# An attention and gated-MLP kernel rewritten: projections one head group ahead, wide normalization, transposes on the DMA queue, a Gelu activation, streamed weights

## The chip, the cores and the metric

The kernel runs on one core of one Trainium2 chip. The metric is the device time of one execution, in microseconds. In the profile, PE is TensorE (matmuls), PEld its weight loads, DVE is VectorE, ACT is ScalarE, POOL is GpSimd and SP is SyncE, which here only issues DMAs. "PEclk" or "clock" is the TensorE clock granted, as a share of full speed.

## The reference

Two pre-norm blocks on 2048 tokens of width 1024, in bf16. Cut to what matters:

```python
def _A_ref(x, wq, wk, wv, wo, beta):          # 32 heads of 32, 4 segments of 512 tokens
    q, k, v = x @ wq, x @ wk, x @ wv          # split into heads and segments
    for s in range(4):
        logits = q_s @ k_s.T * scale + causal_mask
        a_dot = softmax(logits) @ v_s
        a_mem = (phi(q_s) @ M) / (phi(q_s) @ z + 1e-6)   # phi(t) = t+1 if t>0 else exp(t)
        o_s = g * a_mem + (1 - g) * a_dot                # g = sigmoid(beta), one per head
        M, z = M + phi(k_s).T @ v_s, z + sum(phi(k_s))
    return o @ wo
def _B_ref(x, w_in, w_sp, b_sp, w_out):
    z = gelu_tanh(x @ w_in)                   # 1024 -> 3584
    z1, z2 = z[..., :1792], layernorm(z[..., 1792:])
    return (z1 * (w_sp @ z2 + b_sp)) @ w_out  # w_sp: 2048 x 2048 over tokens
h = x + _A_ref(layernorm(x)); out = h + _B_ref(layernorm(h))
```

## The kernel before

Work on each engine is one queue in program order; semaphores join the queues. Four stages follow each other: segment 0 is projected; then for each segment eight groups ("quads") of four heads, with the projections of the next segment as filler, and an output projection at the end of the segment; then the gated input projection; then the spatial product and the output. PV is the product of the exponentials with the values. A bank is one of the eight pieces of the memory in which TensorE leaves its results. z1 and z2 are the two halves of the gated input projection; a z2 chunk is one tile of 128 tokens by 1792 columns.

The logits of one block of keys; the causal mask is added by matmuls with a constant:

```python
def L(j):                                   # j = 0..3, widths 512, 384, 256, 128
    for i in range(4):                      # four heads, four row groups, banks 0-3
        pe.matmul(bank(i)[:, 0:nj], kT[32*i:..., keys j], qT[32*i:..., 128*j:512], start=True, stop=False)
    for i in range(4):
        pe.matmul(bank(i)[:, 0:128], IDENT, NEGTRI, start=False, stop=True)
    act.activation(ESALL[:, :, OFFJ[j]:...], PS[:, 0:4, 0:nj], Exp, scale=SCALE)
# ... PV_emit(cq) for each of four query blocks, then on VectorE, each on 128 columns or fewer:
    dM += eps; RD = 1/[dA, dM]; RD *= GG; TA = A*RD; TM = Mn*RD; otok = TA + TM   # six small operations
```

One block of the gated input projection, on two buffers of each kind. The factor 2 that remains in z is taken out later:

```python
w = [bank free] ; if z2 block and fb == 0: w.append(z2g_res.free)   # previous chunk normalized
tp = proj8(...)                                                     # 8 matmuls, 512 columns
t1 = act.activation(X2T[g], ps, Square)
t2 = dve.scalar_tensor_tensor(WG[g], X2T[g], GELU_K, ps, add, mult)
t3 = act.activation(TH[g], WG[g], Tanh, scale=GELU_C)               # one block later
t4 = dve.scalar_tensor_tensor(out, TH[g], 1.0, ps, add, mult)
# after four z2 blocks: layer norm of the 1792 columns in Z2G, a single buffer
```

The softmax here doesn't subtract the row's maximum and nothing guards it: scores larger than these inputs give would overflow.

Of the kernel before, what the change touches and what calls it, by code (L numbers as in the profile page):

```python
# [5 lines left out]
BF16 = mybir.dt.bfloat16  # L6
# [5 lines left out]
T = 2048  # L12
D = 1024
H = 32
DH = 32
# [6 lines left out]
SCALE = DH ** (-0.5)  # L22
LN_EPS = 1e-5
MEM_EPS = 1e-6
GELU_C = 0.7978845608028654 * 0.044715
GELU_K = 1.0 / 0.044715
NJ = [512, 384, 256, 128]
OFFJ = [0, 512, 896, 1152]
ESLOT = 1280


class _Sig:

    def __init__(self, sem, name):
        self.sem = sem
        self.name = name
        self.n = 0


class _Plan:  # L40
    ENG = ("pe", "act", "dve", "pool", "sp")

    def __init__(self):
        self.ops = {k: [] for k in self.ENG}
        self.waited = {k: {} for k in self.ENG}

    def op(self, eng, fn, waits=(), sig=None):
        w = []
        for item in waits:
            if item is None:  # L50
                continue
            s, v = item
            if v <= 0:
                continue
            if self.waited[eng].get(s.name, 0) >= v:
                continue
            self.waited[eng][s.name] = v
            w.append((s.sem, v))
        semobj = None
        if sig is not None:  # L60
            sig.n += 1
            semobj = sig.sem

        def run(e, fn=fn, w=tuple(w), semobj=semobj):
            for (sm, v) in w:
                e.wait_ge(sm, v)
            ins = fn(e)
            if semobj is not None:
                ins.then_inc(semobj, 1)

        self.ops[eng].append(run)
        return (sig, sig.n) if sig is not None else None

    def dma(self, eng, dst, src, sem16, waits=(), transpose=False):
        w = []
        for item in waits:
            if item is None:
                continue
            s, v = item
            if v <= 0:  # L80
                continue
            if self.waited[eng].get(s.name, 0) >= v:
                continue
            self.waited[eng][s.name] = v
            w.append((s.sem, v))
        sem16.n += 1

        def run(e, dst=dst, src=src, w=tuple(w), semobj=sem16.sem, transpose=transpose):
            for (sm, v) in w:
                e.wait_ge(sm, v)  # L90
            e.dma_start(dst, src, transpose=transpose).then_inc(semobj, 16)

        self.ops[eng].append(run)
        return (sem16, sem16.n)


class _DmaSig(_Sig):
    pass


def _w16(tok):
    if tok is None:
        return None
    s, v = tok
    return (s, 16 * v) if isinstance(s, _DmaSig) else (s, v)


def bass_sequential_preLN__memory_aug_infini_attn__mixer_gmlp__prompt_kernel(
# [16 lines left out]
    plan = _Plan()  # L125
    P = plan.op

    sem_handles = []

    def mksig(name, dma=False):  # L130
        h = nc.alloc_semaphore(name)
        sem_handles.append(h)
        return (_DmaSig if dma else _Sig)(h, name)

    g_pool = mksig("g_pool")
    g_dve_pe = mksig("g_dve_pe")
    g_dve_act = mksig("g_dve_act")
    g_dve_sp = mksig("g_dve_sp")
    g_dve_pool = mksig("g_dve_pool")
    g_dve_dve = mksig("g_dve_dve")  # L140
    g_act_dve = mksig("g_act_dve")
    g_act_pe = mksig("g_act_pe")
    g_act_act = mksig("g_act_act")
    g_pe_act = mksig("g_pe_act")
    g_pe_dve = mksig("g_pe_dve")
    d_w3 = mksig("d_w3", True)
    d_wo = mksig("d_wo", True)
    d_win = mksig("d_win", True)
    d_wout = mksig("d_wout", True)
    d_beta = mksig("d_beta", True)  # L150
    d_x = [mksig("d_x0", True), mksig("d_x1", True)]
    d_xr = [mksig("d_xr0", True), mksig("d_xr1", True)]
    d_hr = [mksig("d_hr0", True), mksig("d_hr1", True)]
    d_wsp = [mksig("d_wsp0", True), mksig("d_wsp1", True)]
    d_brow = [mksig("d_brow0", True), mksig("d_brow1", True)]
    d_out = [mksig("d_out0", True), mksig("d_out1", True)]

    ARENA = 209920 + 2048
    arena = nc.alloc_sbuf_tensor("arena", [128, ARENA], mybir.dt.uint8)
    abase = nc.lookup_mloc(arena).addr  # L160
    _cur = [0]

    def region(size):
        off = _cur[0]
        _cur[0] += size
        assert _cur[0] <= ARENA, ("arena overflow", _cur[0])
        return off

    def tens(name, shape, dt, off):
        sz = int(np.prod(shape[1:])) * mybir.dt.size(dt)  # L170
        assert off % 32 == 0, (name, off)
        assert off + sz <= ARENA, (name, off, sz)
        return nc.alloc_sbuf_tensor_at(name, list(shape), dt, offset=abase + off)

    R_CONST = region(4096)
    R_WQKV = region(49152)
    R_PK = region(16384)
    R_WO = region(16384)
    R_XNT = region(8192)
    R_QT = region(16384)  # L180
    R_KT = region(16384)
    R_PQT = region(16384)
    R_V = region(17408)
    R_E = region(10240)
    R_OTOK = region(8192)
    R_OT = region(8192)
    R_XCH = region(4096)
    R_XN = region(2048)
    R_XR = region(4096)
    R_HCH = region(4096)  # L190
    R_QTMP = region(4096)
    R_NORM = region(4096)
    R_XN2 = region(2048)
    assert _cur[0] == ARENA

    c = R_CONST
    IDENT = tens("ident", [128, 128], BF16, c); c += 256
    TRI = tens("tri", [128, 128], BF16, c); c += 256
    GG = tens("gg", [128, NQ, 8], F32, c); c += 256
    BETAB = tens("betab", [128, H], BF16, c); c += 64  # L200
    G32 = tens("g32", [128, 2, H], F32, c); c += 256
    MSUM = tens("msum", [128, NQ, 33], F32, c); c += 1056
    c = (c + 31) // 32 * 32
    MZ = tens("mz", [128, NQ, 34], BF16, c); c += 544
    STATS = tens("stats", [128, 4, 6], F32, c); c += 96
    MV = tens("mv", [128, 2], F32, c); c += 32
    SM4 = tens("sm4", [128, 8], F32, c); c += 32
    MHALF = tens("mhalf", [128, 1], F32, c); c += 32
    RD = tens("rd", [128, 8], F32, c); c += 32
    SUMS = tens("sums", [128, 8], F32, c); c += 32  # L210
    IOT = tens("iot", [128, 128], I32, c); c += 512
    NEGTRI = tens("negtri", [128, 128], BF16, c); c += 256
    assert c <= R_CONST + 4096

    WQKV = tens("wqkv", [128, 3, 8, D], BF16, R_WQKV)
    PKS = [tens("pk0", [128, 4, D], BF16, R_PK), tens("pk1", [128, 4, D], BF16, R_PK + 8192)]
    WO = tens("wo", [128, 8, D], BF16, R_WO)
    XNT = tens("xnT", [128, 8, L], BF16, R_XNT)
    QTS = [tens("qT0", [128, NQ, L], BF16, R_QT), tens("qT1", [128, NQ, L], BF16, R_QT + 8192)]
    KTS = [tens("kT0", [128, NQ, L], BF16, R_KT), tens("kT1", [128, NQ, L], BF16, R_KT + 8192)]  # L220
    PQTS = [tens("pqT0", [128, NQ, L], BF16, R_PQT), tens("pqT1", [128, NQ, L], BF16, R_PQT + 8192)]
    VS = [tens("v0", [128, 4, H, 34], BF16, R_V), tens("v1", [128, 4, H, 34], BF16, R_V + 8704)]
    ES = [tens("e%d" % i, [128, ESLOT], BF16, R_E + i * 2560) for i in range(4)]
    ESALL = tens("eall", [128, 4, ESLOT], BF16, R_E)
    OTOK = [tens("otok%d" % i, [128, D], BF16, R_OTOK + i * 2048) for i in range(4)]
    OT = tens("oT", [128, NQ, L], BF16, R_OT)
    XCH = [tens("xch%d" % i, [128, D], BF16, R_XCH + i * 2048) for i in range(2)]
    XN = [tens("xn0", [128, D], BF16, R_XN), tens("xn1", [128, D], BF16, R_XN2)]
    XR = [tens("xr%d" % i, [128, D], BF16, R_XR + i * 2048) for i in range(2)]
    HCH = [tens("hch%d" % i, [128, D], BF16, R_HCH + i * 2048) for i in range(2)]  # L230
    TMPE = tens("tmpe", [128, D], BF16, R_QTMP)
    QE = tens("qe", [128, L], BF16, R_QTMP + 2048)
    TA = tens("ta", [128, 4, 32], F32, R_NORM)
    TM = tens("tm", [128, 4, 32], F32, R_NORM + 512)
    MZBD = [tens("mzbd%d" % i, [128, 512], BF16, R_NORM + 1024 + i * 1024) for i in range(2)]

    WIN_LO = tens("w_in_lo", [128, 8, FH], BF16, R_WQKV)
    WIN_HI = tens("w_in_hi", [128, 8, FH], BF16, R_WQKV + 28672)
    HNT = [tens("hnT0", [128, 8, L], BF16, R_WO), tens("hnT1", [128, 8, L], BF16, R_WO + 8192)]
    Z1T = tens("z1T", [128, 14, T], BF16, R_XNT)  # L240
# [17 lines left out]
    WSPCH[1] = tens("wspch1", [128, T], BF16, R_CT2 + 5120)  # L258

    PS = nc.alloc_psum_tensor("ps", [128, 8, 512], F32)  # L260

    def bank_f32(b):
        return PS[:, b, :]

# [792 lines left out]
```

## Time and profile before

Median 1267.4 us (1266.9 to 1271.2, 4 runs). Stages of the profiled execution (1264.5 us):

| stage | us |
|---|---|
| start: weights, projections of segment 0 | 71 |
| attention, projections of segments 1 to 3, output projections | 507 |
| layer norm of h, gated input projection | 351 |
| spatial product and output (22 us of it getting started) | 335.5 |

The page of before: busy time by engine, then busy tenths of TensorE and its clock in 40 slices of the span.

```profile
PE 978.3 (77%) x6735; PEld 490.3 (39%) x6848; DVE 672.3 (53%) x1688; ACT 361.8 (29%) x502; POOL 35.1 (3%) x68
...
PE   3978785888669856674858676758639999999998
...
PEclk9979897998879986567978888889869999999999
```

TensorE is nearly full only in the last ten slices, and in most of the slices in which it is not full its clock is lower too (not in the first).

Busy time by window, before. Columns: window, its length, busy us (and instructions) of each engine, clock, DMA share, GB/s.

```profile
core 0: us, PE busy (x) PEld busy (x) DVE busy (x) ACT busy (x) POOL busy (x), PEclk, DMA share, GB/s
0.00:71.00 71.00, 48.16 (x248) 23.68 (x254) 22.50 (x48) 18.69 (x29) 8.31 (x22) 1.00 0.39 141
71.00:578.00 507.00, 381.94 (x3850) 207.92 (x3906) 281.65 (x984) 216.03 (x233) 8.15 (x14) 0.83 0.11 37
578.00:598.00 20.00, 4.61 (x34) 3.41 (x36) 12.09 (x29) 0.00 (x0) 2.20 (x4) 0.60 0.29 93
598.00:929.00 331.00, 234.27 (x1035) 106.48 (x1053) 234.56 (x449) 125.96 (x239) 15.33 (x28) 0.86 0.03 9
929.00:951.00 22.00, 7.51 (x65) 6.87 (x67) 7.50 (x11) 1.13 (x3) 1.12 (x1) 0.50 0.82 296
951.00:1264.50 313.50, 301.81 (x1508) 141.90 (x1533) 113.95 (x168) 0.00 (x0) 0.00 (x0) 0.99 0.15 47
```

In attention TensorE idles 125 of 507 us at a clock of 0.83; in the input projection it idles 97 of 331 us. The timeline inside that stage shows: the four operations of one block follow each other across two engines, and a block comes every 1.99 us (644.47 to 646.46), while its 8 matmuls need 8 x 0.217 = 1.74 (a run of 8 matmuls of 512 columns takes 1.74 us in this trace; 0.217 is used for one throughout).

```profile
644.47 0.63 ACT L828 ACTIVATE th_117<-wg_115 128x512 bf16<-128x512 bf16 x1 [0.87 <-DVE wg_115 L862]
645.01 0.58 ACT L860 ACTIVATE x2t_111<-ps 128x512 bf16<-128x512 f32 x1
645.14 0.69 DVE L833 SCALAR_TENSOR_TENSOR z1T<-th_117,ps 128x512 bf16<-128x512 bf16 x1
645.74 0.68 DVE L862 SCALAR_TENSOR_TENSOR wg_114<-x2t_111,ps 128x512 bf16<-128x512 bf16 x1
646.46 0.63 ACT L828 ACTIVATE th_116<-wg_114 128x512 bf16<-128x512 bf16 x1 [0.87 <-DVE wg_114 L862]
```

The chain that ended last, by engine, before:

```profile
PE 48%; DVE 31%; ACT 11%; issue 4%; DMA 4%; POOL 2%; SPq 0%; DVEq 0%; ACTq 0%; POOLq 0%
```

### The profile page before, as it was taken

How to read it: one execution, taken by the hardware profiler on the slowest of the kernel's cores; microseconds unless marked ns; L12 is line 12 of the kernel's file. 1: busy time of each engine (PE TensorE's matmuls, PEld its weight loads, DVE VectorE, ACT ScalarE, POOL GpSimd, SP SyncE). 2: the span in 40 equal slices, each digit the busy share in tenths (PEclk: the TensorE clock that was granted, in tenths of full speed). 3: DMA queues.
4: the chain of work that ended last, by engine and by line, in shares of the span. 5: the costliest groups of instructions: out<-in, count | busy, mean ns of one | idle time of the engine just before them, and what ended most of it. 6: DMA issues, size and time to landing. Idle time of an engine off the chain costs nothing.

```text
span 1264.5 us, 16478 instructions
## 1 busy us (share of the span) xinstructions
PE 978.3 (77%) x6735; PEld 490.3 (39%) x6848; DVE 672.3 (53%) x1688; ACT 361.8 (29%) x502; POOL 35.1 (3%) x68
## 2 busy tenths in 40 slices
PE   3978785888669856674858676758639999999998
PEld 1444443443334423332423233323224445444443
DVE  4165426864577425654676777776644434244242
ACT  0357523663146405520334243334410000000000
POOL 2000000000000000000000000000000000000000
PEclk9979897998879986567978888889869999999999
DMA  8000012000300070002000000000042030120201
GB/s 315 1 26 1 1 34 68 1 1 1 101 1 2 2 282 18 1 18 91 18 17 1 17 18 9 9 1 1 1 179 83 5 109 26 50 88 5 68 1 59
DMA packets 23308, 54.56 MB, mean 43 GB/s; under 512 B 2368, under 2 KB 6976, under 8 KB 23232
## 3 DMA queue, kind: packets, MB, share of 16 engines
q1 hardware_dynamic: 19152, 34.10, 8.3%
q0 software_dynamic: 4080, 19.40, 4.1%
q8 instruction: 54, 0.88, 0.3%
q14 instruction: 22, 0.18, 0.0%
HBM read 45.10 MB, written 8.39 MB: 42 GB/s over the span
## 4 chain that ended last, share of the span: by engine, by line
PE 48%; DVE 31%; ACT 11%; issue 4%; DMA 4%; POOL 2%; SPq 0%; DVEq 0%; ACTq 0%; POOLq 0%
PE ps L391 16%; PE ps L945 15%; PE ps L972 8%; DVE stats L328 5%; ACT eall L525 4%; DVE z2g L833 3%; DVE z1T L833 3%; ACT th_116 L828 3%; DVE wg_114 L862 3%; DVE wg_115 L862 3%; ACT th_117 L828 3%; PE ps L518 2%; PE ps L511 2%; POOL sm_58 L333 2%; DMA wqkv<-in_A_wv_dram 2%
## 5 line engine op out<-in xcount | busy, mean ns | idle before, releaser
L525 ACT ACTIVATE eall<-ps 128x2048 bf16<-128x2048 f32 (+3 forms) x128 | 158.6, 1239 | 170.8 <-PE ps L518 170.1
L391 PE MATMUL ps<-xnT,wqkv 128*128 128x512 bf16 x489 | 118.8, 388 | 11.4 <-DVE msum L640 4.5
L972 PE MATMUL ps<-w_out,yT 128*128 128x512 bf16 x437 | 96.8, 379 | 6.9 <-DVE yT L951 6.4
L948 DVE TENSOR_TENSOR tmpg<-ps,brow_126 128x512 f32<-128x512 f32 x56 | 38.7, 691 | 117.5 <-PE ps L945 102.6
L945 PE MATMUL ps<-wspT_119,z_106 128*128 128x512 bf16 x439 | 98.2, 384 | 1.7 <-DVE wspT_119 L922 1.3
L945 PE MATMUL ps<-wspT_120,z_106 128*128 128x512 bf16 x440 | 96.6, 379 | 0.4
L391 PE MATMUL ps<-w_in_hi,hnT_104 128*128 128x512 bf16 (+1 forms) x253 | 63.1, 416 | 36.2 <-DVE z_106 L791 36.1
L391 PE MATMUL ps<-w_in_hi,hnT_103 128*128 128x512 bf16 (+1 forms) x251 | 63.4, 419 | 31.4 <-DVE z_106 L791 29.7
L391 PE MATMUL ps<-wo,oT 128*128 128x512 bf16 x248 | 63.4, 410 | 21.6 <-DVE oT L657 21.4
L828 ACT ACTIVATE th_116<-wg_114 128x512 bf16<-128x512 bf16 (+1 forms) x60 | 36.9, 615 | 134.9 <-DVE wg_114 L862 134.9
L391 PEld LDWEIGHTS ps<-xnT,wqkv 128*128 128x128 bf16 x512 | 47.4, 99 | 62.8 <-DVE msum L640 5.7
L972 PEld LDWEIGHTS ps<-w_out,yT 128*128 128x128 bf16 x448 | 43.5, 98 | 60.2 <-DVE yT L951 8.2
L945 PEld LDWEIGHTS ps<-wspT_119,z_106 128*128 128x128 bf16 x448 | 43.9, 99 | 53.2 <-issue 2.5
L945 PEld LDWEIGHTS ps<-wspT_120,z_106 128*128 128x128 bf16 x448 | 43.7, 98 | 51.9
L391 PE MATMUL ps<-wqkv,xnT 128*128 128x512 bf16 x248 | 58.7, 390 | 3.4 <-DVE msum L640 2.6
L518 PE MATMUL ps<-negtri,ident 128*128 128x128 bf16 x512 | 61.3, 255 | 0.0
L391 PEld LDWEIGHTS ps<-w_in_hi,hnT_104 128*128 128x128 bf16 x256 | 27.8, 111 | 73.2 <-DVE z_106 L791 39.6
L391 PE MATMUL ps<-hnT_103,w_in_lo 128*128 128x512 bf16 x218 | 52.4, 396 | 3.2 <-DVE z2g L833 3.0
L391 PEld LDWEIGHTS ps<-w_in_hi,hnT_103 128*128 128x128 bf16 x256 | 28.1, 112 | 68.3 <-DVE z_106 L791 32.7
L828 ACT ACTIVATE th_117<-wg_115 128x512 bf16<-128x512 bf16 (+1 forms) x60 | 35.2, 587 | 67.4 <-DVE wg_115 L862 67.4
L391 PE MATMUL ps<-hnT_104,w_in_lo 128*128 128x512 bf16 x217 | 51.1, 388 | 1.7 <-DVE z2g L833 1.3
L577 DVE TENSOR_SCALAR ps<-ps 128x4 f32<-128x4 f32 x96 | 16.1, 167 | 67.4 <-PE ps L556 64.4
(145 smaller groups left out, 1313.3 us busy)
## 6 DMA issues: line engine op xcount, KB each, us to landing
wspch_121<-in_B_w_sp_dram SPq DMA_DIRECT2D x8, 512.0 KB, 4.2
wspch_128<-in_B_w_sp_dram SPq DMA_DIRECT2D x8, 512.0 KB, 4.3
hr_0_127<-out_dram SPq DMA_DIRECT2D x16, 256.0 KB, 2.8
w_in_lo<-in_B_w_in_dram POOLq DMA_DIRECT2D x1, 3584.0 KB, 12.4
w_in_hi<-in_B_w_in_dram POOLq DMA_DIRECT2D x1, 3584.0 KB, 21.5
w_out<-in_B_w_out_dram POOLq DMA_DIRECT2D x1, 3584.0 KB, 17.9
xch_87<-in_A_x_dram SPq DMA_DIRECT2D x8, 256.0 KB, 2.8
xch_88<-in_A_x_dram SPq DMA_DIRECT2D x8, 256.0 KB, 3.0
```

Of the source, the lines that this page charges most:

```text
L328: t = P("dve", (lambda e, ci=ci: e.bn_stats(STATS[:, ci, :], eng_in_ap[:, ci * csz:(ci + 1) * csz])), waits=((list(first_wait) + [chain["l ...
L333: tp = P("pool", lambda e: e.tensor_tensor(SM4[:, 1:2], SM4[:, 0:1], MHALF[:], ALU.pow), waits=[t], sig=g_pool)
L391: tok = P("pe", (lambda e, i=i: e.matmul(dst, lhs_of_i(i), rhs_of_i(i), start=(i == 0), stop=(i == 7))), waits=(waits if i == 0 else []), ...
L511: P("pe", (lambda e, i=i, dst=dst: e.matmul(dst, kT[32 * i:32 * (i + 1), c, j * 128:(j + 1) * 128], qT[32 * i:32 * (i + 1), c, 128 * j:512 ...
L518: tp = P("pe", (lambda e, dstd=dstd: e.matmul(dstd, IDENT[:], NEGTRI[:], start=False, stop=True)), sig=(g_pe_act if i == 3 else None))
L525: ta = P("act", (lambda e: e.activation(dst4, src4, ACTF.Exp, scale=float(SCALE))), waits=wa, sig=g_act_pe)
L828: t3 = P("act", (lambda e, g=g, ncols=ncols: e.activation(TH[g][:, 0:ncols], WG[g][:, 0:ncols], ACTF.Tanh, scale=float(GELU_C))), waits=[p ...
L833: t4 = P("dve", (lambda e, g=g, ncols=ncols, dst=dst, o=prev["out"]: e.scalar_tensor_tensor(o, TH[g][:, 0:ncols], 1.0, dst, ALU.add, ALU.m ...
L862: t2 = P("dve", (lambda e, g=g, ncols=ncols, dst=dst: e.scalar_tensor_tensor(WG[g][:, 0:ncols], X2T[g][:, 0:ncols], float(GELU_K), dst, AL ...
L945: tok = P("pe", (lambda e, sc=sc, fc=fc, dst=dst: e.matmul(dst, Z2[:, sc, fc * 128:(fc + 1) * 128], wb[:, sc, :], start=(sc == 0), stop=(s ...
L948: t1 = P("dve", lambda e, dst=dst: e.tensor_tensor(TMPG[:], dst, BROW[0][:], ALU.add), waits=[tok, _w16(tb), tmpg_res.free], sig=g_dve_pe)
L972: tok = P("pe", (lambda e, fc=fc, half=half, tcl=tcl, dst=dst: e.matmul(dst, YT[:, fc, tcl * 128:(tcl + 1) * 128], WOUT[:, fc, half * 512: ...
```

## The change

The intent is to keep TensorE fed. Nearly all of the file is new, so the diff is given as its core; helper code (a recorder that places the waits) is cut.

```diff
 # --- attention, one of 32 head groups n
-L(0); extra; L(1); PV(0); extra; L(2); PV(1); extra; L(3); PV(2); PV(3); state; rest of extras
+logits(n, 0)                               # keys 0, 512 columns
+proj_qk(n + 1, 1)                          # K of the NEXT group
+pv(n - 1, 2)                               # last part of the previous group, then its norm
+bg_pop()                                   # background: layer norm of an x or h tile
+logits(n, 1)                               # keys 1 and 3 share the banks, one exponential
+proj_qk(n + 1, 0)                          # Q of the next group
+pv(n, 0); logits(n, 2); fill(f3); phi(n + 1); pv(n, 1); bg_pop(); state(n); fill(f4); bg_pop()
+# fill = a value projection, or an output projection of the previous segment
 # --- causal mask
-4 x pe.matmul(bank, IDENT, NEGTRI) for each block of keys
+pool.affine_select(out=d, in_=d, ..., fill=0.0)            # on the exponentials, in SBUF
 # --- normalization: per query block 128 columns -> all four at once
+dve.reciprocal(RD, PVA[:, :, :, 32]); RD *= OMG; TA = PVA * RD (512 columns); ot = TA + TM
 # --- transposes (normalized x, h, attention output, phi(K), spatial weights)
-pe.transpose(...) x8; dve.tensor_copy(dst, bank)
+sp.dma_start_transpose(dst[:, :, tile], src)
 # --- gated input projection, w_in streamed through three buffers
-Square, (x2 + K) * x, Tanh, (1 + t) * x
+act.activation(z, PS[:, b, 0:448], ACTF.Gelu_apprx_tanh); dve.bn_stats(ZST[...], z)
 # --- start
-pool.dma_start of wq, wk, wv, wo; all of segment 0 projected before attention
+act.dma_start of wv (first half), wk, wq, wv (second half), wo; attention starts when group 0 is projected
```

## The prediction

> **What bounds the kernel now** (table of busy time by window):
> - 0 to 71 us: weights land (first projection matmul at 25.9 us, released by the last weight load), then segment 0 is projected alone, 45 us.
> - 71 to 578 us: attention and output projections. TensorE is busy 76 to 82% in segments 0 to 2 at a granted clock of 0.88, and 62% at 0.57 in segment 3, which has no projections to fill with. Per group of four heads the timeline shows 14 to 15 us: TensorE, four exponentials (1.88, 1.45, 1.02, 0.60 us) and 24 small VectorE operations of 0.17 to 0.29 us take turns. Each segment end costs 19 to 25 us for the output projection alone.
> - 578 to 929 us: layer norm with nothing to overlap (28 us), then the gated input projection, 323 us, although its 896 matmuls need 896 x 0.217 = 194 us. The chain of waits runs through VectorE and ScalarE: square, multiply, tanh, multiply, 0.6 to 0.7 us each, on two buffers.
> - 929 to 950 us: waiting for the transposed spatial weights. 950 to 1264 us: TensorE at clock 0.99, 302 of 314 us busy.
>
> **What changes, costed from the trace**
> - Gated input projection: one Gelu activation (0.6 us) replaces four operations (2.6 us). TensorE (1.74 us per block) becomes the bound: 194 us, plus the last output projection mixed in (64 x 0.217 = 14 us) and about 9 us of bubbles: 217 instead of 351 (578 to 929).
> - Start: value projections begin when half of one weight has come; the first attention group starts at about 25 us instead of 71.
> - Attention: TensorE per group, from durations: Q and K 3.5, V and output projection 0 to 3.5, logits 1.3, PV 1.6, memory and state 0.9 (estimate): 8.5 in segment 0, 10.7 in 1 and 2, 9.4 in 3. The mask matmuls (0.40 us for four, 16 per group) and transposes leave. ScalarE: 7.6 us; VectorE about 7.3. TensorE-bound with 0.5 to 1 us of bubbles: 345 us, with the output projections inside, instead of 507.
> - Final stage: transposes (16.6 us of TensorE and the 21 us start) go to the DMA queue; 896 + 448 matmuls are 292 us, plus block ends: 303 instead of 335.
> - Added: DMA transposes, some 22 MB, 13 MB of them during attention, about 38 GB/s. The Trainium skill's "Advanced Engine Details and Errata", section X-Bar Transpose, calls them as fast as regular DMAs; no trace here shows one. All have several us of slack in program order. Also four GpSimd selects per group[...], off the chain.
>
> Sum: 25 + 345 + 217 + 303 = 890 us. Nearly all of it is on the critical path, because TensorE becomes the chain.
>
> **Prediction: 890 us, 850 to 955 (8 in 10). Faster by over 2%: 0.97; within 2%: 0.015; slower: 0.015.**
>
> **What would show it.** TensorE busy above 90% in nearly all slices and clock near 1.0; chain of waits over 80% TensorE; input projection stage about 215 us; groups of 9 to 11 us in attention; first exponential at about 25 us.
>
> **What would make it wrong.** DMA transposes far slower than plain copies, or blocking the SyncE queue that issues loads in order (TensorE idle, released by DMA); GpSimd selects of 2 us or more, which would put exponential, select and PV on the chain; the loop through banks 0 to 3 (logits, exponential, logits) or the two spare banks leaving TensorE idle, so that groups stay at 12 us and the clock drops: then 940 to 980.

## More of the kernel before

What TensorE waited for, before (total us, times, longest): the normalization of a z2 chunk, and the exponentials.

```profile
PE ps L391 <- DVE z_106 L791: 65.7, 12, 6.4
PE ps L511 <- ACT eall L525: 50.7, 47, 2.0
```

## The result, and the profile after

After: median 867.3 us (865.7 to 870.2, 4 runs). The ratio to before is 0.684, 95% interval 0.682 to 0.687; ratios can differ a little from the ratio of the medians.

The same lines of the page, after:

```profile
PE 802.0 (93%) x5354; PEld 390.6 (45%) x5440; DVE 382.9 (44%) x777; ACT 302.2 (35%) x351; POOL 121.8 (14%) x234
...
PE   1787988899889999699999999999999999999998
...
PEclk9998999999999999899999999999999999999999
```

Busy time by window, after; the windows are the start, attention, the input projection and the final stage.

```profile
0.00:38.20 38.20, 14.93 (x79) 7.20 (x80) 11.82 (x31) 8.78 (x13) 4.38 (x18) 1.00 0.70 247
38.20:363.50 325.30, 289.77 (x2945) 151.34 (x2992) 203.32 (x483) 225.26 (x219) 101.30 (x176) 0.97 0.33 74
363.50:572.60 209.10, 208.49 (x1014) 100.70 (x1026) 68.71 (x122) 67.59 (x119) 16.13 (x40) 0.99 0.23 58
572.60:865.90 293.30, 288.81 (x1318) 131.41 (x1343) 99.06 (x144) 0.60 (x1) 0.00 (x0) 1.00 0.26 65
```

The chain that ended last, after:

```profile
PE 78%; DVE 7%; ACT 5%; POOL 3%; DMA 3%; ACTq 2%; issue 2%; SPq 1%
```

| stage | before | predicted | after |
|---|---|---|---|
| start | 71 | 25 | 38.2 |
| attention and what it holds | 507 | 345 | 325.3 |
| input projection with layer norm | 351 | 217 | 209.1 |
| final stage | 335.5 | 303 | 293.3 |
| sum | 1264.5 | 890 | 865.9 |

The borders shift work a little: attention now also holds most of segment 0's projections (144 of 192 matmuls, 31 us at 0.217 us each), and the last segment's output projection (64 matmuls, 14 us) went into the input projection stage. In attention TensorE is busy 92 us less, and idles 35.5 instead of 125 us. The input projection idles 0.6 of 209 us. Some matmul records are missing from this trace: its attention has 2945, that of the kernel with four operations below, which has the same attention, has 2992 and shows 294.7 us busy of 322.8. So the 35.5 us may be some 5 too many, and the busy time 5 too few.

Two places are still not full. First, the start. The timeline of after, 2 to 20 us; ACTq lines are the time in which ScalarE's queue sat in issuing a DMA:

```profile
1.92 2.40 ACTq L209 DMA_DIRECT2D wq<-in_A_wq_dram  x1
4.34 7.89 ACTq L209 DMA_DIRECT2D wv<-in_A_wv_dram  x1
12.26 5.31 ACTq L209 DMA_DIRECT2D wo<-in_A_wo_dram  x1
17.60 1.28 ACT L209 ACT_TABLE_LOAD   x1 [17.60 <-issue]
18.89 1.02 ACT L209 ACTIVATE xnT_71<-ps 128x1024 bf16<-128x1024 bf16 x1
19.97 2.32 PE L209 MATMUL ps<-wv,xnT_71 128*128 128x512 bf16 x5 [11.54 <-ACT xnT_71 L209]
```

ScalarE could copy nothing out of a bank before 18.9 us, although TensorE had the first transposed tile done at 8.4 us. Second, the head of a segment. The timeline of after, 115 to 123 us, cut to one chain:

```profile
115.71 1.88 ACT L209 ACTIVATE e_100<-ps 128x2048 bf16<-128x2048 f32 x1
...
115.88 0.58 SPq L209 DMA_DIRECT2D xch_88<-in_A_x_dram  x1
...
118.89 1.42 DVE L209 BATCH_NORM_STATS2 stats_59<-xch_88 128x6 f32<-128x512 bf16 x2 [2.23 <-DMA xch_88<-in_A_x_dram]
...
120.94 0.57 POOL L209 TENSOR_TENSOR rs_63<-rs_63,mhalf 128x1 f32<-128x1 f32 x1
...
121.47 1.40 POOL L209 TENSOR_SCALAR_AFFINE_SELECT e_100<-e_100 128x512 bf16<-128x512 bf16 x2
...
122.16 0.27 PE L209 MATMUL ps<-v,e_100 128*128 128x33 bf16 x4 [1.71 <-POOL e_100 L209]
```

The exponentials were ready at 117.6 us, but their select stood in GpSimd's queue behind the power of a layer norm, which waited for an x tile that had only just been asked for. In all, TensorE waited for selects (the operation on GpSimd that sets the masked exponentials to zero):

```profile
PE ps L209 <- POOL e_100 L209: 16.9, 21, 3.3
```

### The profile page after: what moved, and what is told of

Same layout as the page of the kernel before. It is cut to its first block, busy times and chain, and to the rows that moved or that the text cites. A ratio compares the mean times of both kernels' runs of the same rounds, so it can differ in the third digit from the quotient of the medians.

```text
span 865.9 us, 12541 instructions
## 1 busy us (share of the span) xinstructions
PE 802.0 (93%) x5354; PEld 390.6 (45%) x5440; DVE 382.9 (44%) x777; ACT 302.2 (35%) x351; POOL 121.8 (14%) x234
## 3 DMA queue, kind: packets, MB, share of 16 engines
q1 hardware_dynamic: 117472, 55.60, 26.9%
## 4 chain that ended last, share of the span: by engine, by line
PE 78%; DVE 7%; ACT 5%; POOL 3%; DMA 3%; ACTq 2%; issue 2%; SPq 1%
PE ps L209 78%; ACTq L209 2%; POOL e_100 L209 2%; DMA xch_87<-in_A_x_dram 1%; ACT e_99 L209 1%; DVE stats_59 L209 1%; ACT v L209 1%; ACT e_100 L209 1%; SPq L209 1%; DVE stats_60 L209 1%; DMA xch_88<-in_A_x_dram 1%; ACT etmp L209 1%; POOL rs_63 L209 1%; DVE etmp L209 1%; ACT e_101 L209 0%
## 5 line engine op out<-in xcount | busy, mean ns | idle before, releaser
L209 ACT ACTIVATE e_99<-ps 128x2048 bf16<-128x2048 f32 x32 | 60.0, 1875 | 45.9 <-PE ps L209 45.9
L209 ACT ACTIVATE z_110<-ps 128x448 bf16<-128x448 f32 x64 | 34.8, 543 | 85.2 <-PE ps L209 85.2
L209 ACT ACTIVATE e_100<-ps 128x2048 bf16<-128x2048 f32 x32 | 60.1, 1877 | 0.8 <-PE ps L209 0.7
L209 DVE BATCH_NORM_STATS2 zst<-z_110 128x6 f32<-128x448 bf16 x64 | 39.8, 622 | 41.5 <-ACT z_110 L209 41.5
L209 ACT ACTIVATE z1T<-ps 128x512 bf16<-128x512 f32 x56 | 33.4, 597 | 63.3 <-PE ps L209 63.3
L209 PE MATMUL ps<-wv,xnT_71 128*128 128x512 bf16 x121 | 30.5, 396 | 16.1 <-ACT xnT_71 L209 15.2
L209 POOL TENSOR_SCALAR_AFFINE_SELECT e_100<-e_100 128x512 bf16<-128x512 bf16 x64 | 41.1, 666 | 26.6 <-ACT e_100 L209 26.6
L209 PE MATMUL ps<-v,e_100 128*128 128x33 bf16 x512 | 22.4, 178 | 17.4 <-POOL e_100 L209 16.9
L209 PEld LDWEIGHTS ps<-wo,oT 128*128 128x128 bf16 x256 | 23.7, 99 | 29.4 <-issue 1.9
L209 ACT ACTIVATE e_101<-ps 128x1024 bf16<-128x1024 f32 x32 | 32.7, 1023 | 11.0 <-PE ps L209 10.7
L209 PE MATMUL ps<-xnT_71,wk 128*128 128x512 bf16 x125 | 32.7, 409 | 1.6 <-DVE msum L209 0.9
L209 POOL TENSOR_SCALAR_AFFINE_SELECT e_99<-e_99 128x512 bf16<-128x512 bf16 x32 | 20.5, 639 | 95.7 <-ACT e_99 L209 95.7
L209 PE MATMUL ps<-xnT_72,wk 128*128 128x512 bf16 x126 | 30.0, 380 | 1.3 <-DVE msum L209 0.9
```

The lines of the kernel that those rows point to most:

```text
L209: ins = getattr(e, op.name)(*op.args, **op.kw)
```

## The experiments

Twelve kernels ran. Differences are between medians; before measured 1266.9 to 1268.1 us. Each edit starts from before or after, as named, or from the kernel just shown.

### One part alone: the Gelu activation in before

```diff
-t1 Square; t2 (x2+K)*x; t3 Tanh; t4 (1+t)*x
+t4 = act.activation(out, ps, ACTF.Gelu_apprx_tanh)     # and the factor 2 leaves the layer norm and the end
```

> The kernel before, with one Gelu activation in place of square, multiply, tanh, multiply, and nothing else. Theory A (the four-operation chain on two buffers holds TensorE back): the input projection stage, 323 us, falls to 215 to 240 us and the whole to about 1160 to 1180 us, since the stage then has only its 194 us of matmuls, the small layer norm and a few waits. Rival B (the stage is held by the order of blocks and the serial layer norm of each z2 chunk, not by the chain): the stage stays above 280 us and the whole above 1220 us.

Correct, 1141.0 us against 1268.1: 127 us less. Busy time by window of this kernel, its input projection stage:

```profile
599.00:804.80 205.80, 202.32 (x1056) 99.64 (x1056) 91.60 (x212) 67.63 (x120) 15.33 (x28) 0.99 0.05 14
```

The stage fell from 331 to 206 us and TensorE fills it. Theory A holds; the total came out 19 us below its range, which had the stage at 215 us or more.

### The misplaced wait in before

```diff
-w.append(z2g_res.free)                        # on the first matmul of a z2 chunk
+t4 = dve.scalar_tensor_tensor(..., waits=[t3, z2g_res.free])
```

> The kernel before, with one wait moved: the first matmul of a z2 chunk no longer waits until the previous chunk has been normalized; the VectorE operation that writes the buffer waits for it instead. In the profile of before TensorE idled 65.7 us in 12 such waits. Theory A (the chain of four operations and the VectorE work set the pace, the wait is only where TensorE notices): under 25 us faster, 1245 to 1267 us. Rival B (the misplaced wait itself costs what it shows): 50 to 70 us faster, 1200 to 1215 us.

Correct, 1267.8 us against 1268.1: the same (ratio 0.999, 0.996 to 1.003). What TensorE waited for now:

```profile
PE ps L391 <- DVE z1T L833: 46.5, 12, 6.3
PE ps L344 <- DVE hn L751: 41.8, 7, 11.6
```

Most of the 65.7 us of the first table did not go away; the waits moved to the next place where TensorE meets VectorE. A wait shows where an engine notices that another is late, not what makes it late.

### Undoing it in after: four operations instead of Gelu

```diff
-act.activation(z, PS[:, b, 0:448], ACTF.Gelu_apprx_tanh)
+Square (ACT); (x2+K)*x (DVE); one block later: Tanh (ACT); (1+t)*x (DVE)     # two buffers of each
```

> The kernel after, with the Gelu activation replaced by before's four operations on two buffers of each kind, one block behind; all else as after. Theory A: a block then takes the 1.98 us that it took in before (timeline, 642.5 to 646.5 us) instead of 1.53 or 1.74 us, so the stage of 209 us grows by about 50 us, and the whole is 905 to 930 us; the rest of before's 323 us was the layer norm and hidden-state normalization in front of the chain. Rival: the activations explain all of it, stage above 300 us, whole above 960 us.

Correct, 936.8 us: 69 us more than after, a little above theory A's range. Its input projection stage:

```profile
361.00:638.50 277.50, 226.25 (x1025) 92.54 (x1026) 203.69 (x349) 120.09 (x227) 15.97 (x40) 0.99 0.17 44
```

The same stage cut where the z1 blocks start (518.0) and where their pace becomes even (543.4):

```profile
361.00:518.00 157.00, 119.83 (x576) 53.25 (x576) 120.00 (x211) 58.39 (x115) 9.46 (x24) 0.99 0.21 54
518.00:543.40 25.40, 15.20 (x64) 5.61 (x64) 21.33 (x41) 8.22 (x16) 6.51 (x16) 1.00 0.12 42
543.40:638.50 95.10, 91.22 (x385) 33.67 (x386) 62.36 (x98) 53.48 (x96) 0.00 (x0) 1.00 0.13 28
```

The stage grew by 68 us, not back to 331. So the four operations cost 125 us in the old arrangement and 68 us in the new one. The remaining 57 us I put down to the single z2 buffer with its layer norm in one piece, which seems to cost time only while the chain is late, since with Gelu alone before's stage is as short as after's; no run isolates it. The expected pace of 1.98 us per block is met by the last 48 z1 blocks (95.1 us). But the extra was not spread evenly: the first 8 z1 blocks take 3.2 us each, and the 64 z2 blocks, for each of which VectorE also takes statistics, 143 us (the output projection's 14 taken out), where 8 x 448 columns need 1.5 us per block: 2.2 us on average, 2.4 to 3.2 from 414 us on.

### Without working one group ahead

```diff
+if n > 0: proj_qk(n, 1); proj_qk(n, 0); phi(n)          # at the group's own start
 logits(n, 0)
-proj_qk(n + 1, 1)
 pv(n - 1, 2); bg_pop(); logits(n, 1)
-proj_qk(n + 1, 0)
 pv(n, 0); logits(n, 2); fill(f3)
-phi(n + 1)
```

> The kernel after, with the Q and K projections and the feature map of a head group done at its own start instead of one group ahead; same instructions. Theory A (working one group ahead is what fills the waits for the exponentials): TensorE then idles about 3 us in each of 31 groups (1.7 us behind the first exponential, 1.2 us behind the second): 60 to 120 us slower, 930 to 990 us. Rival (the other fills, PV of the last group, values and output projection, cover the exponentials already): under 30 us slower, below 897 us.

Correct, 1034.1 us: 167 us more, well above theory A's range. Its attention stage, and its waits:

```profile
38.30:531.80 493.50, 359.26 (x2997) 169.77 (x2995) 201.55 (x490) 231.75 (x220) 98.51 (x176) 0.80 0.21 49
```

```profile
PE ps L209 <- ACT e L209: 105.7, 64, 2.2
PE ps L209 <- ACT qk L209: 22.1, 32, 0.7
```

TensorE idles 134 instead of 35.5 us, 99 us more, which is what was expected (3 us in each of 31 groups). But its busy time for the same matmuls also rose by 69 us, at a clock of 0.80. With the records that are missing from after's trace the two parts are nearer 104 and 65 us. The stage is then nearly as long as in before (507 us at 0.83).

### Useless matmuls in those waits

```diff
 pv(n - 1, 2)
+dummy(n, 7)            # 7 matmuls of 512 columns into a spare bank, read by nobody
 ...
 pv(n, 0)
+dummy(n, 5)
 logits(n, 2)
```

> The kernel without the look-ahead (1034 us, granted clock 0.90, TensorE busy 71 us more than in after for the same instructions), with 12 useless matmuls in each group where TensorE waits for the first two exponentials (7 and 5, at most 2.6 us per group at full clock); their results are read by nobody. Theory A (idling costs twice, because the granted clock falls and then all matmuls of the stage are slower): the clock returns above 0.97 and the kernel gets 25 to 70 us faster, 965 to 1010 us, although it computes more. Rival B (only the waits count): the same or up to 30 us slower, 1025 to 1065 us.

Correct, 980.4 us: 54 us faster than without the useless work, still without look-ahead.

```profile
37.90:474.50 436.60, 378.73 (x3376) 176.41 (x3376) 198.82 (x486) 231.31 (x220) 98.35 (x176) 1.00 0.24 55
```

The clock is 1.00. By estimate, the 384 added matmuls are 384 x 0.217 = 83 us of the 379, so the useful ones take about 295 us, where they had taken 359. Theory A is shown: in this kernel idling in short pieces costs TensorE twice, as the wait and as slower matmuls.

### Transposes of 44 tiles back on TensorE

```diff
 def to_T(dst, tcl, src):
-    sp.dma_start_transpose(dst[:, :, tile], src)
+    pe_T(dst, tcl, src)                      # 8 transposes into a bank, one ScalarE copy
```

> The kernel after, with the 44 DMA transposes of normalized inputs, attention outputs and hidden states done on TensorE with a ScalarE copy (1.02 us) out of the bank, as the first four are; the transposes of phi(K) and of the spatial weights stay on the DMA queue. Theory A (TensorE is the chain nearly everywhere, so its work counts in full): 44 x 0.61 = 27 us of TensorE more, 25 to 45 us slower, 892 to 912 us. Rival (TensorE has enough slack in attention, and a DMA transpose's latency of about 3.2 us costs something too): within 10 us of after, 857 to 877 us.

Correct, 996.0 us: 129 us more, about three times the upper end of theory A. The clock of the attention stage fell to 0.90. What TensorE waited for most:

```profile
PE ps L209 <- DVE lno L209: 73.2, 28, 7.4
```

The transposes stand in TensorE's program right behind the VectorE step that makes their input, so TensorE waits for the whole layer norm. The next kernel puts a slot of other work between:

```diff
-bg.append(lambda: pe_T(dst, tcl, ln_apply(src, k)))
+bg.append(lambda: apply); bg.append(lambda: pe_T(dst, tcl, o))     # and the outputs' transposes as tasks too
```

> The 44 transposes on TensorE again, but each placed one background slot (about 3 us of TensorE work) after the VectorE step that makes its input, instead of right behind it. The first form lost 129 us where 25 to 45 had been expected, and TensorE waited 73 us in 28 waits for the normalized tile. Theory A (in TensorE's own program order a transpose drags the latency of load, layer norm and GpSimd power into TensorE; on the DMA queue it waits apart): most of the loss goes, 892 to 925 us. Rival B (the work itself costs it: 27 us of transposes, the lower clock, ScalarE copies and the two spare banks): above 960 us.

919.0 us, but the result is WRONG (relative error 0.30). Walking through its program order shows the cause: with three tasks per tile instead of two in the same number of slots, one of the 44 transposes (the last x tile of segment 3) is recorded after its first reader. All instructions are the same, and one dependency of many is missing, so the time says what it was made for, but a mended form was not run. The wait for the normalized tile fell:

```profile
PE ps L209 <- DVE lno L209: 17.9, 11, 7.1
```

As far as this run tells, 77 of the 129 us were the order, not the work; of these, at least 26 are TensorE's busy time (858.9 to 833.0 us), with the clock back from 0.952 to 0.987. The remaining 52 us are TensorE's added work (833.0 us busy against 802.0, of which by estimate 6 are the records missing from after's trace: 25 us) and more idling. So, if the time of this incorrect kernel is right, most of what the DMA queue buys here is that a transpose waits there without holding TensorE up; the rest is its work. A DMA transpose of 256 KB landed after 3.0 to 3.4 us for most tiles, beside 3.0 to 3.3 for plain loads of x; in after, TensorE has no wait for one in its list of waits.

### The mask on TensorE again

```diff
-pool.affine_select(...)
+4 x pe.matmul(PS[:, i, o:o+128], IDENT, NEGTRI, start=False, stop=True)    # for each block of keys
```

> The kernel after, with the causal mask made by 16 matmuls per group as in before instead of four GpSimd selects (0.63 to 0.68 us each). Theory A (TensorE is the chain; the selects are mostly off it): 32 x 1.6 = 51 us of TensorE more, less the 17 us that TensorE waited for the selects: 30 to 50 us slower, 897 to 917 us. Rival (the selects lie on the chain of exponential, select and PV, and delay more than the waits show): same or faster than after, 850 to 872 us.

Correct, 883.7 us: 16 us more, between the two theories. Its attention stage:

```profile
38.30:380.00 341.70, 319.37 (x3453) 180.14 (x3510) 192.94 (x491) 225.83 (x221) 19.41 (x48) 1.00 0.32 71
```

The 512 matmuls added 29.6 us of busy time net (the clock is also 1.00 instead of 0.97), 0.058 us each, not 51. The 0.40 us for four was read from pieces of the timeline that overlap: in before the four of 237.59 us start while the piece before them, 237.26 and 0.39 long, still runs. Idling fell from 35.5 to 22.3 us.

### Normalization per query block

```diff
-reciprocal, scale, TA, ot on all four blocks; memory part on two
+for q in range(4): the same on one block, 28 operations per group instead of 8
```

> The kernel after, with the softmax and memory normalization done for each of four query blocks on its own, as in before (28 small VectorE operations per group instead of 9 wide ones). VectorE gets about 3.3 us per group more. Theory A (VectorE has slack, but the next PV must wait until the two accumulation banks are read, 3.8 us instead of 1.9 us after the last PV, with about 2.2 us of cover): 20 to 50 us slower, 887 to 917 us. Rival B (fully off the chain): within 8 us. Rival C (the wide normalization is the main gain of attention): over 80 us slower.

(By the edit and the trace it is 28 against 8 from segment 1 on: 552 operations more in all.) Correct, 921.8 us: 54 us more, 5 us above the range of theory A. VectorE's busy time in attention rose by 79 us (203 to 283), and TensorE waited for the reading of the two accumulation banks:

```profile
PE ps L209 <- DVE ta L209: 25.2, 17, 3.7
```

In after that wait is 3.9 us. Wide normalization is worth 54 us, part of it through this wait; TensorE's busy time also rose by 20 us (290 to 310), at a clock of 0.93 instead of 0.97. It is not the main gain of attention.

### Two repairs, apart and together

```diff
-act.dma_start(WV..., WK, WQ, WV..., WO)
+pool.dma_start(WV..., WK, WQ, WV..., WO)
```

> The first half of the faster version alone: weight loads issued from the GpSimd queue instead of the ScalarE queue. First exponential at 27 to 30 us instead of 38.7; 856 to 861 us. If the weights themselves are what the start waits for: no gain.

Correct, 855.3 us (854.2 to 857.6): 12 us less, just below the range expected. The first exponentials start 9.8 us earlier than in after (38.7):

```profile
28.88 1.88 ACT L209 ACTIVATE e<-ps 128x2048 bf16<-128x2048 f32 x1
```

```diff
-x_load(4 * (s + 1) + c)              # in the group that normalizes the tile
+x_load(of the next group's tile)     # one group earlier
```

> The other half alone: each x tile loaded one group earlier. TensorE's waits for selects fall from 17 us to under 6 us; 850 to 858 us. Both halves together gave 843 us, 24 less than after, so the two gains should add up to about 24.

Correct, 853.3 us (850.6 to 854.3): 14 us less. TensorE's wait for selects fell:

```profile
PE ps L209 <- POOL e L209: 5.1, 12, 1.7
```

Both together; this kernel ran before its halves:

> The kernel after with two changes meant to make it faster: the five weight loads at the start are issued from the GpSimd queue instead of the ScalarE queue (in after, ScalarE sat in these issues until 17.6 us, so the first transposed input left its bank only at 18.9 us), and each x tile of the next segment is loaded one group earlier (in after, the GpSimd half of its layer norm waits for the load, and the selects queue behind it: TensorE waits 17 us for selects, and eight or more x loads are on the chain). Expected: first exponential at 27 to 30 us instead of 38.7, i.e. 8 to 12 us less, and 8 to 17 us less in segments 0 to 2: 840 to 852 us. If neither was on the chain: 862 to 870 us.

Correct, 843.4 us (841.0 to 846.8), ratio to before 0.666 (0.664 to 0.668). The halves add up: 12 + 14 = 26 against 24. This version beats both kernels. Its attention stage:

```profile
29.80:339.20 309.40, 283.71 (x2946) 149.67 (x2992) 199.43 (x487) 225.89 (x220) 100.21 (x176) 0.99 0.34 78
```

## Why the prediction was right

The time, 867 us, lies in the range of 850 to 955, 23 us below the point. The direction and mechanism of three stages held; the sizes of four terms were off, and that the sum came so near is partly luck: the misses are 8, 20 and 10 us too many and 13 too few.

- **Input projection, 351 to 217 predicted, 209 measured.** Right in mechanism: the Gelu activation alone in before shortens its stage by 125 us. The 9 us of bubbles were too many: 0.6 us. Not seen: the four operations cost 125 us in before and only 68 in after, so a part of the old loss was the chain together with something else in before's arrangement; that this was the single z2 buffer is not shown.
- **Attention, 507 to 345 predicted, 325 measured.** TensorE per group was over-counted. "8.5 in segment 0, 10.7 in 1 and 2, 9.4 in 3" summed durations of groups of matmuls that overlap each other: in the profile of after, the busy times of the groups in attention, added one by one, give 336 us, against 290 together. (The mask matmuls, costed in the same way at 0.40 us for four, measured 0.23; they are not part of these sums.) Busy time per group was about 8.4, 9.7, 9.8 and 8.4 us (67.0, 77.3, 78.5 and 67.1 us in the windows of the four segments). The bubbles, 0.5 to 1 us per group, were about 1 (1.1 by after's trace, some 0.15 less with the missing records).
- **Start, 71 to 25 predicted, 38 measured.** The failed step is "value projections begin when half of one weight has come": it costed the arrival of data and not the issue. ScalarE, which issued the loads, was held in them until 17.6 us. Moving the issue brings the first exponential from 38.7 to 28.9 us and the whole down by 12 us; some 4 of the missed 13.7 us of that start remain.
- **Final stage, 335.5 to 303 predicted, 293 measured.** Block ends cost about 4.5 us of idling, not 11. That the DMA transposes take away the 22 us start is read from the two profiles; no run undid it alone.
- **Signs named in advance.** "TensorE busy above 90% in nearly all slices" held after attention only, in attention it was 89%; the chain is 78% TensorE, not over 80; the clock is 0.988 over the run; groups take 10.2 us on average, inside 9 to 11; the first exponential is at 38.7, not 25.
- **Selects "off the chain".** At about 0.65 us they were short enough, but not off it: TensorE waited 16.9 us, mostly because they queued behind the layer norm's GpSimd steps. Loading x earlier took away most of these waits.
- **DMA transposes.** They did not hold TensorE up through the SyncE queue, as predicted: SPq is 1% of the chain. What the prediction missed is their main worth: it counted only that the transposes leave TensorE (27 us for 44 tiles, by the estimate in the expectation above), while putting them back right behind their inputs costs 129.
- **The clock.** The prediction treated idle time and matmul time as separate, except in its last line, where the clock drops with longer groups. The look-ahead is worth 167 us, about 99 of idling and 69 of slower matmuls. The Trainium skill, "TensorE: Matmul & The Clock Gate", section "Why this matters for your kernels", warns of idle gaps over about 3 us; here gaps of at most 2.2 us for the exponentials sufficed for a stage average of 0.80.

The gains of the single undoings (167, 129, 69, 54 and 16 us) add to more than the whole 400 us, so they are not shares; presumably each takes away what the others need.

## What to carry to other kernels

In an in-order queue, the place of an instruction decides whose latency it inherits: put work for the next step behind each wait, and move steps that depend on long chains to a queue that may wait (the transposes on TensorE cost 129 us in one place and 52 in another). In this kernel short idle pieces on TensorE also went with a lower clock (0.80 against 1.00 when they were filled), so filling them with work from one group ahead paid more than the idle time shown. Before trusting a wait table, move the wait or the work: the wait that looked like 66 us was worth nothing, and the operations behind it were worth 127.

## What the Trainium skill lacked or had wrong

- "TensorE: Matmul & The Clock Gate" ("Why this matters for your kernels": no idle gaps over about 3 us): as a rule this row is too weak here. Waits of at most 2.2 us for the exponentials, with TensorE busy 73% of the stage, gave an average clock of 0.80 (one other wait in the stage was 3.2 us); filling them with useless matmuls gave 1.00 and 54 us less. Elsewhere the page does say that frequent short idling can lower the clock, without a length; that part agrees.
- "Advanced Engine Details and Errata", X-Bar Transpose ("as fast as regular DMAs", about 90% of a copy): landing agrees for 256 KB (3.0 to 3.4 us against 3.0 to 3.3), less so for 512 KB (5.1 to 5.2 us against 4.2 to 4.3 in before), and DMA engine time does not. By estimate: the SyncE queue took 26.9% of 866 us, 233 us, for 55.6 MB; about 32.5 MB of it are plain, 100 us at before's rate (34.1 MB in 8.3% of 1264.5 us); so the 23 MB of transposes (the sizes of the tiles, added up) took 133 us, 0.17 MB per us against 0.32. Issuing one of at most 256 KB mostly held the queue 1.2 to 1.3 us, a plain load of x 0.33 to 0.59.
- "Trainium Kernel Development and Optimization", Key Constraints (issuing DMAs from several engines only saves sequencer time): it does not say that the issuing engine can be held. Three loads of 1 to 2 MB held ScalarE for 2.4, 7.9 and 5.3 us each; issued from GpSimd, the five took 0.9 to 1.1 us each.
